# One scan per chunk, 64x64 quarters for two products, a new order of the masks and a spread weight fetch in a linear-attention and mixture-of-experts kernel

## The chip, the cores and the metric

The kernel runs on one core of one Trainium2 chip. The metric is the device time of one execution in microseconds (us); lower is better. Five engines work side by side and wait for each other by semaphores: TensorE (PE, with its weight loads shown as PEld), VectorE (DVE), ScalarE (ACT), GpSimd (POOL) and SyncE (SP), whose queue issues most of the DMA transfers.

## The reference

The first half is a linear attention with a decaying state, for 4 batches, 8 heads, 768 time steps and a head size of 48; the second half sends each of the 3,072 resulting rows of 384 numbers through one of 8 experts.

```python
for t in range(S):                                  # per batch b and head h
    cur = einsum('bhd,bhe->bhde', u[None] * kt, vt)
    y[:, :, t] = einsum('bhd,bhde->bhe', rt, state + cur)
    state = wt[..., None] * state + einsum('bhd,bhe->bhde', kt, vt)
...
skip = x @ w_skip;  do = skip > 0                   # x: y with the heads side by side
e = argmax(x @ w_gate);  g = softmax(x @ w_gate)[e]
out[do] = x[do] + g * (relu(x @ w1[e]) @ w2[e])     # other rows: out = x
```

## The kernel before

**Attention in chunks.** The time steps of a batch are cut into six chunks of 128, so there are 24 chunks, worked off by a loop over `s` (lines 595 to 660). All eight heads of a chunk lie in one tile: head 2a+g has its 48 channels on partitions 64g to 64g+47, and a = 0 to 3 runs along the free dimension with 128 time steps each. For each chunk the kernel needs the products of the decays w.

- `prep_scan` (265) makes `q`, the running product of w from the end of the chunk, with one VectorE scan over 516 columns. `prep_keys` (281) takes the reciprocal `rq` of q's first column in each of four groups, makes `kq` = k*q on GpSimd and, by a second VectorE scan, `rh`, the running product from the start. `prep_reads` (293) makes `rp` = r * rq * rh in four VectorE instructions, and `rk` = r*k on GpSimd, told by `beside` to start after the last of the four. `prep_check` (307) has ScalarE test w and save q's first column.
- `intra` (315) transposes `kq` on TensorE into a PSUM bank of tag psT (ScalarE copies it to `kt`), and multiplies kq by rp into the two banks `psa[0]`, `psa[1]` in 64x64 quarters (328). `mask` (331) copies each bank to SBUF times a triangular mask on VectorE. 
- `bonus_sums` (339) sums u*r*k over the channels by four 128x128 products with `ubk_sb`, which holds u twice on its diagonal blocks and zeros elsewhere, into bank psB; `bonus` (346) multiplies this by v's transpose `vt` into the output bank `psy` on VectorE.
- `outputs` (373) adds to `psy` the masked scores times v (eight products, 378) and, unless the chunk is the first of its batch, four 128x128 products of the state `sblk` with `rp` (383). `sblk` again holds zeros outside its diagonal blocks. `update` (349) adds kt times v to the state in bank psu, and `carry` (361) scales it on ScalarE and copies it to `sblk` in two halves.
- `evict` (386) copies `psy` to `xT`; `rows_out` (390) turns it back into rows and computes the router's logits in one product with `wgp_sb`; `store` (399) copies them out and writes the rows to DRAM.

**Order.** The order on every engine is written by hand (`manual_schedule`): each engine takes its instructions in the order in which the loop issues them. In step `s` the loop stores chunk s-1, updates the state and makes the outputs of chunk s, does the scores, masks, bonus sums and bonus of chunk s+1 and the scans of chunk s+2, and issues the loads of chunk s+4. VectorE's order in a step is therefore scan q, rq, scan rh, rp (chunk s+2), two masks, bonus (chunk s+1). TensorE's is update, outputs (s), transposes, scores, bonus sums (s+1), rows_out (s).

**Router and weights beside it.** After each six chunks a generator `router` (412) is dripped between the other steps, `pace` steps at a time. For the first two groups the one-hot rows are made on ScalarE (`mark`, 479), for the others on VectorE (`one_hot`, 474). Expert weights are fetched in pieces of 1024 columns, one piece a step, at the loop's end (652); they are split into two parts, the high part on ScalarE and the low one on GpSimd (273), one slice a step.

**Queues.** `load_chunk` (140) issues for each chunk two DMAs for w, r and k into one of three buffers and two for `vt` into one of four; `load_v` (157) one for v by rows. With the store and a weight piece all of these go through the SP queue in the order of the loop.

**Experts.** After the loop an early part of expert 0 runs beside the last router group (`early_expert`, 563), and then the experts' products follow (739).

## Time and profile before

| | us |
|---|---|
| median of 3 runs | 317.33 |
| lowest and highest run | 316.35, 317.79 |
| the profiled execution's own time | 317.5 |
| span of the profile (first to last instruction) | 315.6 |
| DVE busy in the span | 244.8 (78%) |
| ACT busy in the span | 185.3 (59%) |
| POOL busy in the span | 115.5 (37%) |

The execution's own time is 1.9 us above the span: what lies before the first and after the last instruction. In 40 slices of the span (7.9 us each), the page gives the busy share of each engine in tenths:

```profile
PE   7499999899898998979999999999999999999992
...
DVE  8899999999999999999637479587785949496310
ACT  4437667689775998766633358274564828184200
POOL 8164455555535566543401772411102020101111
```

The attention takes the first half of the slices, the experts the second. A busy PE is not a PE at its peak, since matmuls are pipelined. The chain of work that ended last, which the next part uses, follows each instruction back to what released it.

### The profile page before, as it was taken

The page shows a single profiled execution, that of the slowest core. Times are in us where ns is not written, and L with a number is a line of the kernel's source. Part 1 is how long each engine was busy: PE and PEld are TensorE (multiplying, and loading weights), DVE is VectorE, ACT ScalarE, POOL GpSimd, SP SyncE. Part 2 cuts the span into 40 slices and gives each one's busy share as a digit, 9 for nine tenths or more (in the row PEclk, how much of TensorE's full clock was granted, in tenths as well). Part 3 has the DMA queues.
Part 4 walks back from the last instruction along what each step waited for, and adds up shares of the span by engine and source line. Part 5 has one row for each costly group of instructions (what it writes and reads, how often), then busy time and mean ns, then how long its engine had stood idle before and what let it go on. Part 6 is the DMA issues. An engine that isn't in the chain of part 4 may idle for free.

```text
span 315.6 us, 8456 instructions
## 1 busy us (share of the span) xinstructions
PE 292.2 (93%) x3229; PEld 269.6 (85%) x3229; DVE 244.8 (78%) x505; ACT 185.3 (59%) x527; POOL 115.5 (37%) x118
## 2 busy tenths in 40 slices
PE   7499999899898998979999999999999999999992
PEld 2388888788787887868889899999999999999991
DVE  8899999999999999999637479587785949496310
ACT  4437667689775998766633358274564828184200
POOL 8164455555535566543401772411102020101111
PEclk9879999999999999999999999999999999999998
DMA  7999999999899988885301489756657473630001
GB/s 227 220 214 241 232 292 271 257 264 264 212 233 257 267 187 179 180 206 194 116 25 34 143 294 348 275 195 218 213 199 239 152 256 95 243 143 27 6 4 37
DMA packets 23778, 60.45 MB, mean 192 GB/s; under 512 B 4902, under 2 KB 11338, under 8 KB 23728
## 3 DMA queue, kind: packets, MB, share of 16 engines
q1 hardware_dynamic: 21248, 53.69, 62.6%
q0 software_dynamic: 2048, 5.48, 5.3%
q8 instruction: 27, 0.44, 0.7%
q10 hardware_dynamic: 432, 0.66, 0.6%
q14 instruction: 23, 0.19, 0.2%
HBM read 52.76 MB, written 7.86 MB: 192 GB/s over the span
## 4 chain that ended last, share of the span: by engine, by line
PE 72%; DMA 13%; DVE 10%; POOL 1%; issue 1%; ACT 1%; SPq 0%; POOLq 0%; DVEq 0%
DMA wrk<-wrk 10%; PE psO L790 7%; PE psO L788 7%; PE psO L789 7%; PE psY L378 6%; PE psH L770 6%; PE psH L769 6%; PE psH L768 6%; PE psA L328 6%; PE psY L383 5%; PE psB L343 5%; DVE asb L334 4%; PE psH L126 4%; DVE psY L347 3%; PE psT L321 3%; DVE rp L297 2%
## 5 line engine op out<-in xcount | busy, mean ns | idle before, releaser
L775 ACT ACTIVATE hh<-psH 128x256 fp32r<-128x256 f32 x60 | 23.0, 383 | 56.8 <-PE psH L770 53.5
L732 POOL DMA_INDIRECT out<-fin,ids x16 | 17.0, 1065 | 102.5 <-DVE fin L795 94.7
L770 PE MATMUL psH<-xTh,w1l 128*128 128x256 f32 x168 | 47.6, 283 | 0.0
L769 PE MATMUL psH<-xTl,w1h 128*128 128x256 f32 x168 | 47.6, 283 | 0.0
L768 PE MATMUL psH<-xTh,w1h 128*128 128x256 f32 x168 | 47.6, 283 | 0.0
L302 POOL TENSOR_TENSOR rk<-wrk 128x512 f32<-128x512 f32 x24 | 30.6, 1275 | 28.9 <-DVE rp L297 14.5
L788 PE MATMUL psO<-w2h,hh 128*128 128x384 f32 x120 | 40.8, 340 | 0.0
L790 PE MATMUL psO<-w2h,hl 128*128 128x384 f32 x120 | 40.2, 335 | 0.0
L789 PE MATMUL psO<-w2l,hh 128*128 128x384 f32 x120 | 40.2, 335 | 0.0
L378 PE MATMUL psY<-asb,v 128*48 128x128 f32 x384 | 26.6, 282 | 13.1 <-DVE psY L347 13.0
L287 POOL TENSOR_TENSOR kq<-wrk,q 128x512 f32<-128x512 f32 x24 | 28.6, 1190 | 18.5 <-DVE q L277 13.4
L776 DVE SCALAR_TENSOR_TENSOR hl<-psH,hh 128x256 fp32r<-128x256 f32 x60 | 25.2, 420 | 12.5 <-ACT hh L775 12.1
L334 DVE TENSOR_TENSOR asb<-psA,c_sb 128x512 f32<-128x512 f32 x48 | 30.7, 681 | 4.3 <-PE psA L328 4.3
L378 PEld LDWEIGHTS psY<-asb,v 128*48 128x48 f32 x384 | 20.5, 126 | 15.6 <-DVE psY L347 15.4
L297 DVE SCALAR_TENSOR_TENSOR rp<-wrk,rq,rh 128x128 f32<-128x128 f32 x96 | 33.1, 405 | 0.5
L770 PEld LDWEIGHTS psH<-xTh,w1l 128*128 128x128 f32 x168 | 32.2, 192 | 0.0
L769 PEld LDWEIGHTS psH<-xTl,w1h 128*128 128x128 f32 x168 | 32.2, 192 | 0.0
L768 PEld LDWEIGHTS psH<-xTh,w1h 128*128 128x128 f32 x168 | 32.2, 192 | 0.0
L795 DVE SCALAR_TENSOR_TENSOR fin<-psO,gates,xg 128x384 f32<-128x384 f32 x15 | 9.3, 618 | 28.5 <-PE psO L790 28.5
L289 DVE TENSOR_TENSOR_SCAN rh<-wrk,pss 128x516 f32<-128x516 f32 x24 | 28.9, 1205 | 2.6 <-PE pss L516 1.3
L277 DVE TENSOR_TENSOR_SCAN q<-wrk,pss 128x516 f32<-128x516 f32 x24 | 29.1, 1214 | 1.4 <-DMA wrk<-wrk 1.4
L343 PE MATMUL psB<-rk,ubk_sb 128*128 128x128 f32 x192 | 27.8, 288 | 0.9 <-POOL rk L302 0.9
(145 smaller groups left out, 668.6 us busy)
## 6 DMA issues: line engine op xcount, KB each, us to landing
r<-w SPq DMA_DIRECT2D x48, 512.0 KB, 5.8
wrk<-wrk SPq DMA_DIRECT2D x46, 288.9 KB, 6.3
v<-vN SPq DMA_DIRECT2D x24, 192.0 KB, 6.2
out<-x SPq DMA_DIRECT2D x24, 192.0 KB, 5.4
vt<-wrk SPq DMA_DIRECT2D x46, 96.0 KB, 6.1
wrk<-wrk SPq DMA_DIRECT2D x1, 258.5 KB, 3.8
wrk<-wrk ACTq DMA_DIRECT2D x1, 256.0 KB, 4.0
wrk<-wrk SPq DMA_DIRECT2D x1, 256.0 KB, 4.5
```

The lines of the kernel that those rows point to most:

```text
L277: nc.vector.tensor_tensor_scan(q.rearrange("p a j -> p (a j)")[:, ::-1], t[:, 1:1 + NP * CW][:, ::-1], floor, 0.0, op0=ALU.mult, op1=ALU.max)
L297: last = nc.vector.scalar_tensor_tensor(rp[:, a], wk["r"][:, a], wk["rq"][:, a], wk["rh"][:, a, :P], op0=ALU.mult, op1=ALU.mult)
L302: mul = nc.gpsimd.tensor_tensor(rk.rearrange("p a j -> p (a j)"), wk["w"][:, R_OFF:K_OFF], wk["w"][:, K_OFF:V_OFF], op=ALU.mult)
L334: nc.vector.tensor_tensor(s, psa[g], tri.rearrange("p (o j) -> p o j", o=1).to_broadcast([P, NP, P]), op=ALU.mult)
L343: nc.tensor.matmul(wk["psb"][:, a], ubk_sb[:, a], wk["rk"][:, a], start=True, stop=True)
L378: nc.tensor.matmul(psy[64 * g:64 * g + D, a], v[:, 2 * a + g], wk["asb"][g][:, a], start=False, stop=(c == 0), skip_group_check=True)
L768: nc.tensor.matmul(ps, w1h[:, o:o + P], xTh[:, kc], start=(kc == 0), stop=False)
L769: nc.tensor.matmul(ps, w1h[:, o:o + P], xTl[:, kc], start=False, stop=False)
L770: nc.tensor.matmul(ps, w1l[:, o:o + P], xTh[:, kc], start=False, stop=(kc == KC - 1))
L788: nc.tensor.matmul(pso, h[j, fc][0], w2h[:, o], start=(fc == 0), stop=False)
L789: nc.tensor.matmul(pso, h[j, fc][0], w2l[:, o], start=False, stop=False)
L790: nc.tensor.matmul(pso, h[j, fc][1], w2h[:, o], start=False, stop=(fc == FC - 1))
```

## The change

**One scan.** The scan `rh`, the small reciprocal `rq` and the four instructions of `rp` go. `prep_keys` takes the reciprocal of all 512 columns of q into `rp`, and `prep_reads` multiplies `rp` by r in place.

```diff
-            nc.vector.reciprocal(rq, wk["q"][:, :, 0:1])
+            rp = wk["rp"] = att.tile([P, NP, P], F32, tag="rp", name=f"rp{i}", bufs=3)
+            nc.vector.reciprocal(rp, wk["q"][:, :, :P])
...
-            nc.vector.tensor_tensor_scan(
-                rh.rearrange("p a j -> p (a j)"), wk["w"][:, 0:NP * CW], floor, 0.0,
-                op0=ALU.mult, op1=ALU.max)
...
-            for a in range(NP):
-                last = nc.vector.scalar_tensor_tensor(
-                    rp[:, a], wk["r"][:, a], wk["rq"][:, a], wk["rh"][:, a, :P],
-                    op0=ALU.mult, op1=ALU.mult)
+            last = nc.vector.tensor_tensor(rp, rp, wk["r"], op=ALU.mult)
```

**Quarters.** `ubk_sb` and `sblk` lose their zero blocks, and the two products that used them become eight products each, of 64 partitions (half g) into 64 output partitions (half c2). Heads are therefore laid out anew: bank `psY`+g holds the heads of half g, with a = 2*c2 + a2. The bonus sums lose their own bank and go into those halves of the score banks' columns that `psb` names.

```diff
-            for a in range(NP):
-                nc.tensor.matmul(wk["psb"][:, a], ubk_sb[:, a], wk["rk"][:, a],
-                                 start=True, stop=True)
+        psb = [z.rearrange("p a (h j) -> p a h j", h=2)[:, :, 1] for z in psa]
...
+            for a2 in range(2):
+                for c2 in range(2):
+                    for g in range(2):
+                        a, rows = 2 * c2 + a2, slice(64 * g, 64 * g + HP)
+                        nc.tensor.matmul(psb[g][64 * c2:64 * c2 + HP, 2 * a2:2 * a2 + 2],
+                                         ubk_sb[rows, a], rk[rows, a], start=True, stop=True)
...
-            nc.vector.tensor_tensor(psy, work[i]["psb"], vt_sb[i % (NBUF + 1)], op=ALU.mult)
+            for g in range(2):
+                work[i]["bonus"] = nc.vector.tensor_tensor(
+                    psy[g][:, :2 * P].rearrange("p (q j) -> p q j", j=HP), psb[g],
+                    vt[:, 4 * g:4 * g + 4], op=ALU.mult)
...
-                for a in range(NP):
-                    nc.tensor.matmul(psy[:, a], sblk[i % 2][:, a], wk["rp"][:, a],
-                                     start=False, stop=True, skip_group_check=True)
+                for a2 in range(2):
+                    for c2 in range(2):
+                        for g in range(2):
+                            a, rows = 2 * c2 + a2, slice(64 * g, 64 * g + HP)
+                            nc.tensor.matmul(psy3[g][64 * c2:64 * c2 + D, a2],
+                                             sblk[i % 2][rows, a, :D], wk["rp"][rows, a],
+                                             start=False, stop=True, skip_group_check=True)
```

With this, `carry` copies the state in one instruction instead of two halves, `evict` copies two half banks, `store` puts its columns back in order, `vt` is loaded by four DMAs of half the size (`load_vt`, one step later than before), and `wgp_sb` by twelve DMAs instead of three in step -2.

**Order.** In step s the bonus sums and the bonus are those of chunk s, not s+1; the transposes (`turn`) are cut off from the scores; `prep_reads` comes behind the masks; `rows_out` of chunk s-1 opens the step.

```diff
                 if on(s - 1):
+                    rows_out(s - 1)
                     store(s - 1)
+                if on(s):
+                    update(s)
+                    carry(s)
+                    bonus_sums(s)
+                drip(pace[0])
...
+                if on(s):
+                    bonus(s)
                 if on(s + 2):
                     prep_scan(s + 2)
+                if on(s + 1):
+                    turn(s + 1)
+                flush()
                 if on(s):
                     outputs(s)
-                flush()
                 if on(s + 2):
                     prep_keys(s + 2)
                     drip(2 * pace[0])
-                    prep_reads(s + 2)
                 if on(s):
                     evict(s)
                 if on(s + 1):
-                    intra(s + 1)
+                    scores(s + 1)
+                    drip(2 * pace[0])
                     mask(s + 1, 0)
                     mask(s + 1, 1)
-                    bonus_sums(s + 1)
-                    bonus(s + 1)
-                    drip(2 * pace[0])
+                if on(s + 2):
+                    prep_reads(s + 2)
                 if on(s + 2):
                     prep_check(s + 2)
```

**Weights and router.** Weight pieces go out at the steps in `FETCH` (k = s - 3) instead of three steps in a row; the slices' split starts one or two steps later. All one-hot rows are made on VectorE (`mark` goes), and the last paces are 3 instead of 2. GpSimd's low part of a slice now waits for the bonus of chunk s instead of the last router instruction.

```diff
+FETCH = (((0, 1), (0, 2, 4)), ((1, 0), (9, 11, 13)), ((0, 0), (10, 12, 14)), ((1, 1), (18, 19, 20)))
...
-                for eq, k0 in (((0, 1), 0), ((0, 0), 3), ((1, 0), 8), ((1, 1), 16)):
-                    if k == k0:
+                for eq, at in FETCH:
+                    if k == at[0]:
                         gens[eq] = load_weights(*eq)
-                    if k0 <= k < k0 + 3:
+                    if k in at:
                         next(gens[eq])
-                if 1 <= k < 7:
-                    split_slice(0, 5 + k, nc.gpsimd)
-                if 9 <= k < 15:
-                    split_slice(1, k - 9, nc.gpsimd)
+                if 2 <= k < 8:
+                    split_slice(0, 4 + k, nc.gpsimd)
+                if 11 <= k < 17:
+                    split_slice(1, k - 11, nc.gpsimd)
```

More of the change, by code (lines that the diff above doesn't have):

```diff
@@ L153, in load_chunk, with load_vt @@
                 nc.sync.dma_start(t[64 * g:64 * g + D], wrk[b, c, g, :, :V_OFF])
-            for g in range(2):
-                nc.sync.dma_start(vf[64 * g:64 * g + D], wrk[b, c, g, :, V_OFF:V_OFF + NP * P])
+        def load_vt(i):
+            b, c = seq[i]
+            vt = vt_sb[i % (NBUF + 1)]
+            for c2 in range(2):
+                for g in range(2):
+                    o = V_OFF + 2 * c2 * P
+                    nc.sync.dma_start(vt[64 * c2:64 * c2 + D, 2 * g:2 * g + 2],
+                                      wrk[b, c, g, :, o:o + 2 * P])
         def load_v(i):
@@ L165, in rwkv_moe_kernel @@
         c_sb = keep.tile([P, C_W], F32, name="c_sb")
-        ubk_sb = keep.tile([P, NP, P], F32, name="ubk_sb")
+        ubk_sb = keep.tile([P, NP, HP], F32, name="ubk_sb")
         u_sb = keep.tile([P, NP], F32, name="u_sb")
@@ L186, in rwkv_moe_kernel @@
         psu = ps1.tile([P, NP, HP], F32, tag="psu", name="psu")
-        psy = ps1.tile([P, NP, P], F32, tag="psY", name="psY")
+        psy = [ps1.tile([P, 512], F32, tag=f"psY{g}", name=f"psY{g}") for g in range(2)]
+        psy3 = [z[:, :2 * P].rearrange("p (b j) -> p b j", b=2) for z in psy]
         psa = [ps1.tile([P, NP, P], F32, tag=f"psA{g}", name=f"psA{g}") for g in range(2)]
-        sblk = [pers.tile([P, NP, 2, HP], F32, name=f"sblk{i}") for i in range(2)]
+        sblk = [pers.tile([P, NP, HP], F32, name=f"sblk{i}") for i in range(2)]
         ohs = keep.tile([P, 1, E], BF16, name="ohs")
@@ L235, in setup @@
             nc.gpsimd.memset(key, 0.5)
-            for g in range(2):
-                rows = slice(64 * g, 64 * g + HP)
-                nc.scalar.copy(ubk_sb[rows, :, rows],
-                               u_sb[rows].rearrange("p (a o) -> p a o", o=1)
-                               .to_broadcast([HP, NP, HP]))
-            nc.tensor.matmul(psy.rearrange("p a j -> p (a j)"), warm[:, :P], warm,
-                             start=True, stop=True, skip_group_check=True)
+            nc.scalar.copy(ubk_sb, u_sb.rearrange("p (a o) -> p a o", o=1)
+                           .to_broadcast([P, NP, HP]))
+            for z in psy:
+                nc.tensor.matmul(z, warm[:, :P], warm, start=True, stop=True,
+                                 skip_group_check=True)
             nc.tensor.matmul(psu.rearrange("p a j -> p (a j)"), warm[:, :P], warm[:, :NP * HP],
                              start=True, stop=True, skip_group_check=True)
-        later, held, marks = deque(), [], deque()
+        later, held = deque(), []
         def flush():
@@ L272, in prep_scan @@
                 lo, raw, hi = lows.pop(0)
-                mul = nc.gpsimd.tensor_tensor(lo, raw, hi, op=ALU.subtract)
-                if vec.last is not None:
-                    beside(mul, vec.last)
+                beside(nc.gpsimd.tensor_tensor(lo, raw, hi, op=ALU.subtract), work[i - 2]["bonus"])
             q = wk["q"] = att.tile([P, NP, CW], F32, tag="q", name=f"q{i}")
@@ L323, in intra, with scores @@
                 nc.scalar.copy(kt, pst)
+        def scores(i):
+            wk = work[i]
             for a in range(NP):
@@ L368, in carry @@
             nb = sblk[(i + 1) % 2]
-            for g in range(2):
-                rows = slice(64 * g, 64 * g + HP)
-                nc.scalar.copy(nb[rows, :, g, :D], psu[rows, :, :D])
+            nc.scalar.copy(nb[:, :, :D], psu[:, :, :D])
         def outputs(i):
@@ L393, in rows_out @@
             px = psx.rearrange("p a j -> p (a j)")
-            for a in range(NP):
-                o = (a // 2) * X2 + (a % 2) * 2 * D
-                nc.tensor.matmul(px[:, o:o + XW], xT[:, a], wgp_sb[:, a], start=(a == 0),
-                                 stop=(a == NP - 1), skip_group_check=True)
+            for q in range(4):
+                o = (q // 2) * X2 + (q % 2) * 2 * D
+                nc.tensor.matmul(px[:, o:o + XW], xT[:, q], wgp_sb[:, q], start=(q == 0),
+                                 stop=(q == 3), skip_group_check=True)
         def store(i):
@@ L574, in early_expert @@
                 hfs.append((h0l[:, fs], hf, h0h[:, fs].bitcast(F32)))
-            pso = ps1.tile([P, DM], F32, tag="psB", name="psO0")
+            pso = ps1.tile([P, DM], F32, tag="psY1", name="psO0")
             w2h, w2l = wsp[0, 2], wsp[0, 3]
@@ L752, in expert @@
             for q in range(nh):
-                ps = ps1.tile([P, CAP], F32, tag=("psA0", "psA1", "psY", "psB")[q % 4],
+                ps = ps1.tile([P, CAP], F32, tag=("psA0", "psA1", "psY0", "psY1")[q % 4],
                               name=f"psH{e}_{q}")
```

130 lines of the change are left out of this document (58 added, 72 removed).

## The prediction

> **What bounds the kernel now.** I read the page first, then the chain of waits for the extent of the attention, the busy time of that stretch, one step of it, and the DMAs.
>
> ```profile
> span 315.6 us, 8456 instructions
> PE 72%; DMA 13%; DVE 10%; POOL 1%; issue 1%; ACT 1%; SPq 0%; POOLq 0%; DVEq 0%
> ...
> 16.05 1.95 PE psY L378 x16
> ...
> 163.16 0.59 ACT xT L388
> ...
> 16.05:163.16 147.11, 137.82 (x2092) 120.66 (x2093) 135.56 (x280) 105.57 (x345) 75.00 (x69) 0.99 0.90 219
> ```
>
> The chain runs from the first product into `psy` at 16.05 us to the last copy out of it at 163.16: 147.1 us for 24 chunks, 6.13 us each. In this stretch (last row: PE, PEld, DVE, ACT, POOL, clock, DMA share, GB/s) PE is busy for 137.8 us and DVE for 135.6, so two engines are nearly full, and the page's 10% for DVE is no measure of what DVE sets. An undisturbed step, first DVE by the timeline (start, us), then PE by the chain:
>
> ```profile
> 28.27 1.22 DVE L277 TENSOR_TENSOR_SCAN q<-wrk,pss 128x516 f32<-128x516 f32 x1
> 29.52 0.18 DVE L284 RECIPROCAL rq<-q 128x4 f32<-128x4 f32 x1
> 29.62 1.20 DVE L289 TENSOR_TENSOR_SCAN rh<-wrk,pss 128x516 f32<-128x516 f32 x1
> 30.85 1.14 DVE L297 SCALAR_TENSOR_TENSOR rp<-wrk,rq,rh 128x128 f32<-128x128 f32 x4
> 32.35 1.29 DVE L334 TENSOR_TENSOR asb<-psA,c_sb 128x512 f32<-128x512 f32 x2 [0.35 <-PE psA L328]
> 33.55 0.69 DVE L347 TENSOR_TENSOR psY<-psB,vt 128x512 f32<-128x512 f32 x1
> ```
> ```profile
> 29.74 1.09 PE psY L383 x8
> 30.82 0.44 PE psT L321 x4
> 31.26 1.02 PE psA L328 x24
> 32.28 1.09 PE psB L343 x8
> 33.37 0.87 PE psX L396 x8
> 34.24 0.49 PE psu L356 x16
> 34.74 0.88 PE psY L378 x16
> ```
>
> PE's seven groups follow each other without a gap and sum to 5.88 us: that is the period. DVE has 0.35 us to spare in it, so router steps and disturbances push it over, and the mean becomes 6.13. A gain needs both engines to become shorter.
>
> **VectorE.** Start to start, a step now takes 1.25 (scan q) + 0.10 (rq) + 1.23 (rh) + 1.14 (rp) + 1.20 (masks) + 0.60 (bonus) = 5.5 us, the wait aside. Gone are rq, rh and the old rp, 2.47. New are a reciprocal of 512 columns and a product of two SBUF tiles of 512.
>
> ```profile
> L96 DVE TENSOR_TENSOR w1l<-r,w1h 128x512 fp32r<-128x512 f32 x36 | 24.9, 693 | 2.1
> ...
> L205 DVE RECIPROCAL gate<-sm x4: 164/182/191, 64.2 to 167.0; 128x6 f32<-128x6 f32 x4
> ...
> L284 DVE RECIPROCAL rq<-q x24: 178/179/181, 6.4 to 150.2; 128x4 f32<-128x4 f32 x24
> ```
>
> The product has its like in the 0.69 us of L96. The reciprocal is the unknown: the trace has it at 4 columns (178/179/181 ns) and 6 (164/182/191). The medians differ by 3 ns for two columns, 1.5 ns a column: 0.18 + 508 x 1.5 ns = 0.94 us. From 178 to 191 it would be 6.5 ns: 3.5 us, the far end; the near end is no slope at all, 0.18. I take the rate of the nearest large elementwise row, (693 - 179)/508 = 1.0 ns a column, 0.69 us. The bonus becomes two instructions of 256 columns, 0.18 + 252 x 1.0 ns = 0.43 each, 0.77 together with the 0.1 us by which neighbours overlap (rows 29.52 and 29.62). Start to start: 1.25 + 0.60 + 1.20 + 0.60 + 0.70 = 4.35 us.
>
> To this come router steps. They are all on one line, 205, and the same stretch has for that line's DVE time:
>
> ```profile
> 16.05:163.16 147.11, 10.22 (x52) 0.99 0.90 219
> ...
> L205 DVE TENSOR_SCALAR hot<-iota,rall 128x256 bf16<-128x256 bf16 x12 | 2.6, 283 | 0.1
> ```
>
> 10.2 us, with 12 one-hot rows more at 0.28 (the second row), 3.4 us: 13.6/24 = 0.57 a step. DVE: 4.9 us a step.
>
> **TensorE.** Quarter-size products run side by side, but not for nothing. Scores (L328) are 64x64 quarters too: each of the four array quarters gets four streams of 128 columns or of 64, at most 512 columns, in 1.02 us. The weight queue idles where the shape of the products changes, as before L343:
>
> ```profile
> PEld psB L343 <- issue: 3.4, 20, 0.2
> ```
>
> 20 times 0.17 us. So scores are 0.17 + 0.85, 1.66 ns a column with four quarters side by side. Bonus sums give each quarter two streams of 128 columns: 0.43 + 0.17 = 0.60, and the state's part the same, instead of 1.09 each (0.43 to 0.85 are the ends, the full overlap without the shape change and the time of all sixteen scores). The order adds shape changes: rows_out and the transposes now follow quarters (+0.17 each), scores follow the state's quarters and save it. New step: 0.87 + 0.17 (rows_out), 0.49, 0.60, 0.44 + 0.17, 0.88, 0.60, 0.85: 5.07 us.
>
> The Trainium skill, TensorEngine Tiling (Array Packing), Key Properties, says that a change of tiling mode, as against one of tile, drains the engine, and that tiles of one mode run independently; by its four tiles at once without that drain each product would be 0.43 here, and the step 0.5 us shorter. The 0.17 us of the row is the drain's price here, so I keep it.
>
> **The new wait.** Bonus sums share banks with the scores, so they wait for both masks, and everything behind them on PE waits too. Count from the scores' end: masks from 0.07 to 1.35 (two of 0.68, overlapping), and PE does rows_out and update meanwhile, 1.53: the wait is covered by 0.1 us, and would cost what the masks run longer. Bonus sums end at 2.13. DVE does rp until 1.95, then a router step, then the bonus from 2.2: first bank at 2.6, second at 2.96. PE's transposes last until 2.74 and the first bank's products until 3.2, so the second bank is ready. Outputs, state and scores end at 5.07; DVE's scan and reciprocal are then done at 4.9 with router steps behind. Everything fits with 0.1 to 0.2 us to spare, so I add 0.18 for steps where it doesn't: 5.25 a step, 24 x (5.25 - 6.13) = **-21.1 us**.
>
> GpSimd's low part of a weight slice now waits for the bonus, with kq queued behind it: at about the 1.23 us of kq's row further down it runs from 2.96 to 4.2, where the scan's end releases kq anyway, and kq is needed only in the next step. ScalarE loses a half copy and the one-hot rows and gets one more eviction of half the size; with 105.6 us busy in 147 it has room.
>
> **What comes back.** First, DMA. Bytes a chunk (KB each):
>
> ```profile
> r<-w SPq DMA_DIRECT2D x48, 512.0 KB, 5.8
> wrk<-wrk SPq DMA_DIRECT2D x46, 288.9 KB, 6.3
> v<-vN SPq DMA_DIRECT2D x24, 192.0 KB, 6.2
> out<-x SPq DMA_DIRECT2D x24, 192.0 KB, 5.4
> vt<-wrk SPq DMA_DIRECT2D x46, 96.0 KB, 6.1
> ...
> 37.00:57.00 20.00, 19.59 (x314) 17.22 (x312) 19.21 (x42) 14.43 (x48) 10.61 (x9) 1.00 1.04 267
> ```
>
> 2 x 288.9 + 2 x 96 + 192 + 192 KB = 1.18 MB a chunk, 1.71 with a weight piece. In the stretch of six weight pieces in a row DMA moves 267 GB/s at a share of 1.04, full: 4.4 us for a plain step, 6.4 for one with a piece. Spread pieces (steps 3, 5, 7) average 5.4, just hidden. But `FETCH` interleaves two tensors at k = 9 to 14, steps 12 to 17: six pieces in a row again, 6 x (6.4 - 5.25) = 6.9 us of backlog, less some 3 us by which loads run ahead: **+3.9**. The last three pieces meet no chunk loads.
>
> Second, contention of DVE and POOL:
>
> ```profile
> 111.38 2.16 DVE L297 SCALAR_TENSOR_TENSOR rp<-wrk,rq,rh 128x128 f32<-128x128 f32 x4
> 111.63 1.23 POOL L287 TENSOR_TENSOR kq<-wrk,q 128x512 f32<-128x512 f32 x1
> ```
>
> Beside kq the rp group takes 2.16 us, not 1.14. In the new order rp stands behind the masks, where kq is done; the router's one-hot rows can still meet POOL: **+1.5** in all.
>
> Third, the start. SP goes through 2 more `vt` DMAs a chunk and nine more for `wgp_sb`. The queue holds only so many:
>
> ```profile
> 63.95 6.65 DMA wrk<-wrk
> ...
> 70.62 7.75 DMA wrk<-wrk
> ...
> 65.73 0.78 SPq L155 DMA_DIRECT2D vt<-wrk  x2
> 66.60 0.38 SPq L160 DMA_DIRECT2D v<-vN  x1
> 67.07 0.38 SPq L410 DMA_DIRECT2D out<-x  x1
> 67.50 0.44 SPq L90 DMA_DIRECT2D r<-w  x1
> 70.01 0.94 SPq L153 DMA_DIRECT2D wrk<-wrk  x2
> ...
> wgp_sb<-wgp SPq DMA_DIRECT2D x1, 9.0 KB, 4.4
> ```
>
> The load issued at 63.95 lands at 70.60, and the second `wrk` of 70.01 goes out at 70.62: between them lie the other wrk half, two vt, v, out, r and one wrk, so at most eight DMAs are in flight. The smallest of `wgp_sb`'s takes 4.4 us to land (last row), so twelve keep the queue for 12 x 4.4/8 = 6.6 us, and three for 1.7; behind them lie the load of chunk 3 and, by the data, rows_out of chunk 0, which I put 1.5 us late, the rest hidden by the first scores: **+1.5**. The first output itself moves little (one scan less, loads 1 us later).
>
> The experts' part keeps its work. Sum against the profiled execution: 317.5 - 21.1 + 3.9 + 1.5 + 1.5 = **303.3 us**; the median of the runs is 0.2 lower. Forecast 303, and by the step's error of 0.25 us (24 x 0.25 = 6) and the DMA term its own range is 296 to 309.
>
> **Rivals.** (a) **DMA stays the bound.** A chunk has 8 DMAs, 9 with weights, and eight fit. If SP's order or smaller rows keep steps near 5.6 and weight steps near 6.4, the attention takes 12 x 5.6 + 12 x 6.4 = 144 less the pieces without loads, a gain of 1 to 9: 309 to 317. For it: the share of 1.04, and 6 us to landing. Against: most of that time is waiting behind other bytes, and the bytes are the same. 0.14.
>
> (b) **The landing time is fixed and not a queue's**: with 8 in flight and 6.3 us each, a plain step is 6.3 us and one with a piece 9/8 x 6.3 = 7.1: 161 us, +14: 331, slower. It decides from 6.1 us a landing. Against: `r` of 512 KB and `vt` of 96 KB would not both need 6 us if bytes didn't queue, but do so behind each other. 0.06.
>
> (c) **The reciprocal is slow.** If the engine needs eight passes for each column, it is 0.18 + 508 x 8 x 1.0 ns = 4.2 us, DVE's step is 8.4, and 24 x (8.4 - 6.13) = +55: about 371. It decides from 1.9 us on (4.9 + 1.2 = 6.1), 3.4 ns a column. For it: 179 ns at 4 columns leave room for 8 ns each. Against: two more columns would add 16 ns, and the medians differ by 3. 0.07. The Trainium skill, VectorE: DVE Perf Modes, First, the fixed hardware budget, says that reciprocal runs as an iterative divide with a repeat count of 8; the two rows speak against eight passes a column, but no row here is wide enough to decide.
>
> (d) **Better than reckoned**, the quarters hide their shape changes and DMA runs ahead: 24 x 5.0 = 120, no backlog: below 296, say 292. 0.08.
>
> (e) The quarters run one after the other: 8 x 128 x 1.66 ns = 1.7 us a product, a step of 7.3, 345. The scores' row excludes it nearly: 0.01.
>
> **Numbers.** Forecast 0.64 (296 to 309), (a) 0.14, (b) 0.06, (c) 0.07, (d) 0.08, (e) 0.01. The range 293 to 316 holds the forecast, most of (a) and half of (d): 0.64 + 0.13 + 0.04 = 0.81. A measurement of this kernel tells 0.5% from no change (315.7 to 318.9). Faster: 0.64 + 0.11 + 0.08 = 0.83; same, the upper edge of (a): 0.03; slower, (b), (c) and (e): 0.14.
>
> **What would show it.** The reciprocal near 0.7 us and rp near 0.69; about 0.6 us for each of the two products in quarters; scores start to scores start about 5.2 us in plain steps; waits of PE for the masks or for the bonus below 0.3 us a step; SP's waits on landings in steps 12 to 17. It is wrong if the reciprocal's row is above 1.9 us, if PE waits over 0.5 us a step for DVE, or if scans wait for `wrk`.

## The result: 15% slower

The changed kernel takes 365.88 us (median of 4 runs, 364.9 to 368.16) beside 317.56 for the kernel before on the same chip: a ratio of 1.154, 95% interval 1.147 to 1.160. The forecast was 303, the range 293 to 316. Further on, a ratio leaves out runs over 1.5% above their kernel's fastest of the same set, which on the chip of e4 to e7 leaves two of the thirteen runs of the kernel before (321.19 and 323.05 us; the others took 326.97 to 328.76), and in e14's later set on that chip all eleven (326.84 to 328.78). From the profile of the changed kernel, first the busy times and the costliest group of the page (behind the bar: busy us in all, mean ns of one, idle us before):

```profile
PE 308.9 (85%) x3582; PEld 272.5 (75%) x3582; DVE 281.3 (77%) x445; ACT 170.3 (47%) x506; POOL 113.5 (31%) x117
...
L285 DVE RECIPROCAL rp<-q 128x512 f32<-128x512 f32 x24 | 80.5, 3353 | 0.8
```

The reciprocal takes 3,353 ns, not 690. A step without router work, by VectorE's timeline (start, us, line, what it makes, in brackets the idle time before it):

```profile
58.08 1.22 DVE L277 TENSOR_TENSOR_SCAN q<-wrk,pss 128x516 f32<-128x516 f32 x1
59.33 3.35 DVE L285 RECIPROCAL rp<-q 128x512 f32<-128x512 f32 x1
62.60 1.22 DVE L331 TENSOR_TENSOR asb<-psA,c_sb 128x512 f32<-128x512 f32 x2
63.74 0.68 DVE L293 TENSOR_TENSOR rp<-rp,wrk 128x512 f32<-128x512 f32 x1
64.64 0.76 DVE L351 TENSOR_TENSOR psY<-psA,vt 128x256 f32<-128x256 f32 x2 [0.21 <-issue]
65.31 1.22 DVE L277 TENSOR_TENSOR_SCAN q<-wrk,pss 128x516 f32<-128x516 f32 x1
```

VectorE is busy nearly without a gap for 7.23 us, scan to scan; before it was 5.88. TensorE now waits for it, and pays twice. Its timeline in this step and the following one:

```profile
63.38 1.16 PE L345 MATMUL psA<-rk,ubk_sb 64*64 64x128 f32 x16 [1.39 <-DVE asb L331]
...
65.23 1.95 PE L384 MATMUL psY<-asb,v 128*48 128x128 f32 x16
...
71.58 1.17 PE L345 MATMUL psA<-rk,ubk_sb 64*64 64x128 f32 x16 [1.28 <-DVE asb L331]
...
73.33 1.08 PE L384 MATMUL psY<-asb,v 128*48 128x128 f32 x16
```

The bonus sums wait 1.39 and 1.28 us for the masks, which stand behind the reciprocal. The same sixteen products then take 1.95 us once and 1.08 the next time: the granted clock reads 0.50 from 65 to 68 us and 1.00 around 73. The mean granted clock of the execution is 0.898 (0.986 before). The last products of `rows_out`, by the view of the tile psX (min/median/max ns, first and last start), for the changed kernel:

```profile
L407 PE MATMUL psX<-wgp_sb,xT x192: 274/275/542, 22.0 to 212.7; 128*128 128x105 f32 x192
```

and for the kernel before:

```profile
L396 PE MATMUL psX<-wgp_sb,xT x192: 255/275/358, 21.4 to 164.7; 128*128 128x105 f32 x192
```

The attention ends 48.0 us later; the profiled executions differ by 366.46 - 317.5 = 49.0. Nearly all of the loss is in the attention.

### The profile page after: what moved, and what is told of

Same layout as the page of the kernel before. It is cut to its first block, busy times and chain, and to the rows that moved or that the text cites. A ratio compares the mean times of both kernels' runs of the same rounds, so it can differ in the third digit from the quotient of the medians.

```text
span 364.7 us, 9180 instructions
## 1 busy us (share of the span) xinstructions
PE 308.9 (85%) x3582; PEld 272.5 (75%) x3582; DVE 281.3 (77%) x445; ACT 170.3 (47%) x506; POOL 113.5 (31%) x117
## 4 chain that ended last, share of the span: by engine, by line
PE 45%; DVE 8%; DMA 1%; issue 1%; POOL 1%; ACT 0%; POOLq 0%; DVEq 0%
PE psO L794 6%; PE psO L795 6%; PE psO L796 6%; PE psH L776 6%; PE psH L775 6%; PE psH L774 6%; DVE rp L285 4%; PE psH L127 3%; PE psX L407 2%; DVE q L277 2%; PE psY L384 1%; PE psX L733 1%; DVE psY L351 1%; DMA xg<-out,idr 1%; PE psA L325 1%
## 5 line engine op out<-in xcount | busy, mean ns | idle before, releaser
L285 DVE RECIPROCAL rp<-q 128x512 f32<-128x512 f32 x24 | 80.5, 3353 | 0.8
L345 PE MATMUL psA<-rk,ubk_sb 64*64 64x128 f32 x384 | 26.2, 324 | 27.7 <-DVE asb L331 22.9
L738 POOL DMA_INDIRECT out<-fin,ids x16 | 17.1, 1066 | 102.5 <-DVE fin L801 94.7
L345 PEld LDWEIGHTS psA<-rk,ubk_sb 64*64 64x64 f32 x384 | 15.7, 154 | 33.9 <-issue 24.3
L384 PE MATMUL psY<-asb,v 128*48 128x128 f32 x384 | 34.6, 337 | 3.8 <-DVE psY L351 3.7
L399 ACT COPY xT<-psY 128x256 f32<-128x256 f32 x48 | 15.7, 376 | 43.0 <-PE psY L392 41.6
L384 PEld LDWEIGHTS psY<-asb,v 128*48 128x48 f32 x384 | 26.4, 153 | 10.7 <-DVE psY L351 10.4
L325 PE MATMUL psA<-rp,kq 64*64 64x128 f32 (+1 forms) x768 | 30.6, 284 | 2.2 <-DVE rp L293 2.2
```

Source lines behind the costliest of these rows:

```text
L285: nc.vector.reciprocal(rp, wk["q"][:, :, :P])
L325: nc.tensor.matmul(psa[g][j:j + HP, a, j:], wk["kq"][rows, a, j:j + HP], wk["rp"][rows, a, j:], start=True, stop=True)
L345: nc.tensor.matmul(psb[g][64 * c2:64 * c2 + HP, 2 * a2:2 * a2 + 2], ubk_sb[rows, a], rk[rows, a], start=True, stop=True)
L384: nc.tensor.matmul(psy3[g][64 * c2:64 * c2 + D, a2], v[:, 2 * a + g], wk["asb"][g][:, a], start=False, stop=(c == 0), skip_group_check=True)
```

## The experiments

Two readings stood against each other. **The reciprocal** alone: everything else gains as forecast. **The rest too**: order, start or DMAs lose what they were to gain. A ratio is always to the kernel before on the same chip, with its 95% interval. Some chips take about 10 us longer than the first in the experts' part: from the last rows_out to the end of the span it is 151 us before and 152 after on the first, 162 in e7 and in m1_widths, which are the kernel before with a small edit, on others. So stretches of the attention are compared in the traces, one profiled execution of each kernel. The table is worked out from the starts of the q scans in each trace (us): when chunk 3's begins, from there to chunk 20's (17 steps), from there to chunk 23's, and the last start of rows_out.

| kernel | scan 3 | 3 to 20 | 20 to 23 | last rows_out | ratio |
|---|---|---|---|---|---|
| before | 22.5 | 106.8 | 19.7 | 164.7 | 1 |
| after | 28.4 | 134.4 | 32.1 | 212.7 | 1.154 |
| e1_two_scans | 27.7 | 110.4 | 28.1 | 180.7 | 1.058 |
| e2_reciprocal_alone | 24.8 | 126.1 | 24.0 | 191.4 | 1.079 |
| e3_max_instead | 28.0 | 103.9 | 28.9 | 175.1 | 1.044 |
| e4_fewer_dmas | 26.0 | 96.7 | 27.7 | 164.8 | 1.019 |
| e9_pieces_in_a_row | 23.9 | 101.6 | 27.7 | 167.4 | 1.007 |
| e10_after_fewer_dmas | 25.6 | 134.4 | 31.5 | 209.5 | 1.141 |
| e13_quarters_products_behind | 22.2 | 100.6 | 25.6 | 161.8 | not settled |
| e14_flush_ahead_of_carry | 23.1 | 102.5 | 21.8 | 160.8 | 0.990 |

### The reciprocal by itself

In m1_widths the kernel before takes five reciprocals more, in `setup`:

```diff
+            for w in (8, 32, 64, 128, 256):
+                nc.vector.reciprocal(sblk[1].rearrange("p a g j -> p (a g j)")[:, :w],
+                                     smask.rearrange("p a j -> p (a j)")[:, :w])
```

> The kernel before with five more reciprocals in the setup, of 8, 32, 64, 128 and 256 columns, into a tile that is cleared afterwards: the cost of a column by itself. If each column costs 6.2 ns at any width (3.35 us less 0.15 over 512), they take 0.20, 0.35, 0.55, 0.95 and 1.75 us; if the slow rate belongs to wide ones or to q's values and strides, the narrow ones stay near 0.2 and the 256 columns near 0.45.

Its groups by shape (behind the first bar: busy us in all, then the mean of one in ns):

```profile
L287 DVE RECIPROCAL rq<-q 128x4 f32<-128x4 f32 x24 | 4.3, 179 | 0.8
L220 DVE RECIPROCAL sblk<-smask 128x256 f32<-128x256 f32 x1 | 1.8, 1753 | 0.0
L220 DVE RECIPROCAL sblk<-smask 128x128 f32<-128x128 f32 x1 | 1.0, 952 | 0.0
L205 DVE RECIPROCAL gate<-sm 128x6 f32<-128x6 f32 x4 | 0.7, 180 | 0.0
L220 DVE RECIPROCAL sblk<-smask 128x64 f32<-128x64 f32 x1 | 0.6, 553 | 0.0
L220 DVE RECIPROCAL sblk<-smask 128x32 f32<-128x32 f32 x1 | 0.4, 353 | 0.0
L220 DVE RECIPROCAL sblk<-smask 128x8 f32<-128x8 f32 x1 | 0.2, 203 | 0.0
```

A straight line: (1753 - 203)/248 = 6.25 ns a column, 153 ns before the first; at 512 columns 3,353 ns, the row of the changed kernel to the nanosecond, and at 4 columns 178. The six-column rows with a median of 182 don't lie on it (191 would), only their maximum does; why the others are shorter no run shows.

In e2_reciprocal_alone the kernel before takes over the reciprocal and the one product, and nothing else:

```diff
-            nc.vector.reciprocal(rq, wk["q"][:, :, 0:1])
-            nc.vector.tensor_tensor_scan(rh...)
+            nc.vector.reciprocal(rp, wk["q"][:, :, :P])
...
-            for a in range(NP):
-                last = nc.vector.scalar_tensor_tensor(rp[:, a], ...)
+            last = nc.vector.tensor_tensor(rp, rp, wk["r"], op=ALU.mult)
```

> The kernel before with only the wide reciprocal and the product by r in place of the small reciprocal, second scan and four instructions; order, full products and fetch as before. Theory R: VectorE's step is 5.5 - 2.47 + 3.35 + 0.60 = 7.0 plus 0.4 for the router, 24 x (7.4 - 6.13) = +30: about 345 to 350. Theory O: near 320, since the old order is kept.

354.24 us, 1.079 (1.075 to 1.083): plain steps of 7.04 us, and the prediction's 5.5 - 2.47 with 3.39 for the reciprocal and 0.61 for the product, start to start, make 7.03. On the chip of this run 1.079 is 26 us; by the traces the attention ends 26.7 us later.

In e1_two_scans the changed kernel gets both scans and the old rp back, behind the masks, and keeps the rest:

```diff
-            nc.vector.reciprocal(rp, wk["q"][:, :, :P])
+            nc.vector.reciprocal(rq, wk["q"][:, :, 0:1])
+            nc.vector.tensor_tensor_scan(rh...)
...
-            last = nc.vector.tensor_tensor(rp, rp, wk["r"], op=ALU.mult)
+            for a in range(NP):
+                last = nc.vector.scalar_tensor_tensor(rp[:, a], ...)
```

> The changed kernel with the first part undone: the small reciprocal, the second scan and the four instructions for rp are back (rp still behind the masks); quarters, order and fetch stay. Theory R (the wide reciprocal, 3.35 us, is what costs): a step of VectorE is 1.25 + 0.10 + 1.23 + 1.14 + 1.20 + 0.60 + 0.57 for the router = 6.1 at most, less where nothing waits; the time comes down by 24 x about 2.2 = 53 us, to 308 to 318. Theory O (the new order, with bonus sums in the score banks behind both masks, costs by itself): it stays above 330.

346.98 us, 1.058 (1.050 to 1.066). So the reciprocal isn't all: without it the rest is still slower than before. In e3_max_instead the reciprocal's place is taken by an instruction of the length that the prediction had reckoned; the division is left out, rp is r times q:

```diff
-            nc.vector.reciprocal(rp, wk["q"][:, :, :P])
+            nc.vector.tensor_tensor(rp, wk["q"][:, :, :P], floor..., op=ALU.max)
```

> The changed kernel with the wide reciprocal replaced by an elementwise maximum of q and the floor in PSUM, 512 columns, about 0.69 us: the division is left out, rp is r times q, and the routing follows other values. It is the cost that the prediction took for the reciprocal. Theory R: what the prediction summed for the rest, 303, plus a start that is some 5 us later than reckoned (the trace of the changed kernel issues chunk 3's load at 22.5 us instead of 14.4): 302 to 310. Theory O: above 320.

341.83 us, 1.044 (1.039 to 1.048), with the stand-in at 0.69 us. **Both readings hold**: the reciprocal takes 37.6 us of the attention (212.7 - 175.1), and what is left is 4.4% slower, not 4.5% faster.

### The DMAs

The chain of waits of e3 near the end (start, us, what):

```profile
125.54 6.32 DMA wrk<-wrk
...
131.93 0.33 SPq L158
...
132.31 6.73 DMA wrk<-wrk
...
139.11 0.33 SPq L158
...
139.49 6.19 DMA wrk<-wrk
```

One load a step stands in the chain: it is issued, lands 6 us later, and only then does SP's queue go on to the next chunk's. In e4_fewer_dmas the same bytes come in fewer DMAs, since the host lays the second copy of v and `wgp` out in the new order:

```diff
-                for g in range(2):
-                    o = V_OFF + 2 * c2 * P
-                    nc.sync.dma_start(vt[64 * c2:64 * c2 + D, 2 * g:2 * g + 2],
-                                      wrk[b, c, g, :, o:o + 2 * P])
+                nc.sync.dma_start(vf[64 * c2:64 * c2 + D],
+                                  wrk[b, c, c2, :, V_OFF:V_OFF + NP * P])
...
+                    nc.sync.dma_start(wgp_sb, wgp)
```

> The kernel of e3_max_instead (its division is still left out), but the host lays the second copy of v and wgp out in the new order, so that a chunk's vt comes in two DMAs instead of four and wgp in one instead of twelve; the bytes are the same. In e3 the step in the middle of the attention was 5.9 us, the scan of chunk 3 started 5.6 us later than before, and the whole was 13.7 us above the kernel before. Theory N (the number of DMAs binds: eight in flight, each some 5 to 6 us from issue to landing, nine or ten to a chunk): steps fall to about 5.3 us (-13 us in 20 steps) and the start gives 4 back: 322 to 328 us, a ratio of 0.98 to 1.0 to the kernel before. Theory B (the bytes bind, 1.2 to 1.7 MB a step): only the start is mended, 336 to 339 us, a ratio of 1.025 to 1.035. A third, W (PE and VectorE take turns around the shared psA banks, and the loop is as long as that chain): also only the start, but then hardly a scan waits for wrk.

328.31 us, 1.019 (1.010 to 1.027). By the traces the attention ends 10.3 us earlier than in e3: 2.0 of them are won ahead of chunk 3, 7.2 in the 17 steps. By the ratios the gain is 2.5%, but e4's stands beside the two shortest runs of the kernel before; beside the median of all thirteen, 327.78, e4 is level. Its plain step on TensorE, products of the outputs to the same products of the next chunk:

```profile
25.86 1.08 PE L381 MATMUL psY<-asb,v 128*48 128x128 f32 x16
26.87 0.65 PE L389 MATMUL psY<-rp,sblk 64*48 64x128 f32 x16
27.34 1.04 PE L322 MATMUL psA<-rp,kq 64*64 64x128 f32 x32
28.31 1.14 PE L404 MATMUL psX<-wgp_sb,xT 128*128 128x105 f32 x8
29.38 0.56 PE L359 MATMUL psu<-v,kt 128*48 128x48 f32 x16
29.88 0.67 PE L342 MATMUL psA<-rk,ubk_sb 64*64 64x128 f32 x16
30.48 0.66 PE L312 MATMUL psT<-c_sb,kq 128*128 128x128 f32 x4
31.14 1.08 PE L381 MATMUL psY<-asb,v 128*48 128x128 f32 x16
```

The groups follow each other without a gap, 5.28 us in all. Its five steps from chunk 3 to 8 take 5.17 to 5.29 us each, beside the forecast's 5.25. e7_before_more_dmas does the opposite to the kernel before:

```diff
-                nc.sync.dma_start(vf[64 * g:64 * g + D], wrk[b, c, g, :, V_OFF:V_OFF + NP * P])
+                for h in range(2):
+                    nc.sync.dma_start(vf[64 * g:64 * g + D, 2 * h * P:2 * (h + 1) * P],
+                                      wrk[b, c, g, :, V_OFF + 2 * h * P:V_OFF + 2 * (h + 1) * P])
```

> The kernel before with one edit: each chunk's vt comes in four DMAs of half the width instead of two (eight and nine DMAs a chunk instead of six and seven), the same bytes. Theory N: eight in flight at 5 to 6 us each give a step of 5.5 to 6.5 us, so steps with a weight piece become later and the kernel takes 3 to 9 us more (a ratio of 1.01 to 1.03). Theory B: no difference that can be measured (0.997 to 1.004).

331.77 us, 1.020 (1.005 to 1.035); by the traces the attention ends 3.3 us later (168.0): in the direction of the number of DMAs. Both edits also halve or double the length of a row that a DMA moves, so the runs don't tell whether it is the eight in flight or the smaller rows.

e9_pieces_in_a_row is e4 with the old fetch of the weights:

```diff
-FETCH = (((0, 1), (0, 2, 4)), ((1, 0), (9, 11, 13)), ((0, 0), (10, 12, 14)), ((1, 1), (18, 19, 20)))
+FETCH = (((0, 1), (0, 1, 2)), ((0, 0), (3, 4, 5)), ((1, 0), (8, 9, 10)), ((1, 1), (16, 17, 18)))
```

> The kernel of e4_fewer_dmas with the weights fetched as in the kernel before (three pieces in a row, at steps 0, 3, 8 and 16 after the first, and the slices split as there). Plain steps of e4 take 5.28 us, those of chunks 9 to 12 and 14 to 18 take 5.6 to 6.4, beside spread pieces. Theory S (the interleaved spread costs, as the prediction had it with 3.9 us): 3 to 6 us below e4, a ratio of 1.0 to 1.01. Theory B (the bytes cost the same in any order): within 2 us of e4.

320.13 us, 1.007 (1.004 to 1.011). By the ratios it gains about 3.5 us on e4, whose ratio rests on two runs of the kernel before; by the traces it loses 4.9 in the 17 middle steps and gains 2.2 ahead of chunk 3, where no weight is fetched yet, and its attention ends 2.6 later. The two chips differ by more than that, so the effect of the spread is not settled; a loss of the spread's in the middle is not to be seen.

e10_after_fewer_dmas gives the changed kernel itself, reciprocal and all, the layout of e4 (the diff above).

> The changed kernel itself, reciprocal and all, with the host's layout of e4 (two DMAs for vt, one for wgp): the full computation. Theory R (the reciprocal's 3.35 us make VectorE the bound, and the DMAs lie beside it): steps stay at 7.2 to 8.2 us, only the start gains, a ratio of 1.14 to 1.155 (the changed kernel has 1.154). Theory A (the two losses add up, since e4 took 13.5 us off e3): a ratio of 1.10 to 1.12.

362.49 us, 1.141 (1.135 to 1.146): 3.2 us at the end of the attention, 2.8 of them won ahead of chunk 3, where the same edit brought 10.3 beside the quick stand-in. While VectorE needs 7.2 us a step, the loads have time. The losses don't add up: each bound hides a part of the other.

### The router in the queues

e4 takes 27.7 us for its last three steps, the kernel before 19.7. VectorE of e4, with the router in its queue:

```profile
135.42 1.28 DVE L328 TENSOR_TENSOR asb<-psA,c_sb 128x512 f32<-128x512 f32 x2
136.62 0.68 DVE L290 TENSOR_TENSOR rp<-rp,wrk 128x512 f32<-128x512 f32 x1
138.94 0.41 DVE L503 TENSOR_TENSOR sg<-oh,vals 128x240 bf16<-128x240 bf16 x1 [1.64 <-POOL vals L500]
139.26 0.76 DVE L348 TENSOR_TENSOR psY<-psA,vt 128x256 f32<-128x256 f32 x2
139.93 1.22 DVE L273 TENSOR_TENSOR_SCAN q<-wrk,pss 128x516 f32<-128x516 f32 x1
```

and TensorE:

```profile
137.34 0.66 PE L312 MATMUL psT<-c_sb,kq 128*128 128x128 f32 x4
141.20 0.19 PE L510 MATMUL pss<-tab,identb 128*128 128x40 bf16 x1 [3.20 <-DVE q L273]
...
141.75 1.95 PE L381 MATMUL psY<-asb,v 128*48 128x128 f32 x16
143.63 1.10 PE L389 MATMUL psY<-rp,sblk 64*48 64x128 f32 x16
144.52 1.92 PE L322 MATMUL psA<-rp,kq 64*64 64x128 f32 x32
```

A router step waits for GpSimd; the bonus stands behind it. A router product waits for the scan, which reads `floor` in the same bank; the outputs, ready 1.2 us earlier, stand behind it. Then the products run at half the clock: the busy times of a plain stretch and of that one (last three columns: granted clock, DMA share, GB/s; the plain one is the last chunk of a batch, which has no update):

```profile
41.70:46.88 5.18, 5.18 (x92) 4.09 (x93) 4.63 (x9) 2.93 (x12) 2.35 (x3) 1.00 1.06 291
141.82:146.43 4.61, 4.61 (x66) 3.90 (x65) 0.84 (x2) 1.57 (x6) 0.94 (x2) 0.50 0.02 4
```

(2.5 us of e4's excess belong to the stand-in, which reads that bank too and waited 1.82 and 0.72 us for router copies and products.) The following runs move this work. e5_router_later is e4 with the router's steps behind the scan and behind rp:

```diff
-                drip(pace[0])
...
                     prep_scan(s + 2)
+                drip(pace[0])
...
-                    drip(2 * pace[0])
                     mask(s + 1, 0)
                     mask(s + 1, 1)
                 if on(s + 2):
                     prep_reads(s + 2)
+                if on(s + 1):
+                    drip(2 * pace[0])
```

> As e4_fewer_dmas, and the router's steps moved behind the scan and behind rp, so that none stands ahead of the masks or the bonus in VectorE's queue (in e3 the last four scans came 28.9 us after one another where before they took 19.7, with router steps of 1.5 us ahead of the masks and 1.6 us of waiting ahead of the bonus). Theory W (what stands ahead of masks and bonus lengthens the loop one for one): 5 to 9 us below e4. Theory V (VectorE's sum is what counts, and it doesn't matter where a step stands): within 2 us of e4.

334.47 us, 1.028 (1.014 to 1.042); in the profiled run, of 329.12 us, the attention is as long as in e4 (164.9): moving alone brings nothing. e8_router_behind puts them behind the outputs and behind rp, and the cast of iota on GpSimd two steps later, out of the way of chunk 1's kq; the stand-in is q times r:

```diff
                     outputs(s)
+                drip(pace[0])
...
                     prep_reads(s + 2)
+                if on(s + 1):
+                    drip(4 * pace[0] if on(s + 2) else 2 * pace[0])
...
+                if s == 0:
                     nc.gpsimd.tensor_copy(iota, c_sb[:, C_IOTA:C_IOTA + 2 * P])
```

> The kernel of e4_fewer_dmas with its order mended where its trace shows losses against the kernel before: the scan of chunk 3 starts 3.6 us later (GpSimd's first kq stands behind a cast of iota that waits for a load, and TensorE's first outputs stand behind the transposes that wait for kq), and the last three scans take 8.0 us longer (router steps ahead of masks and bonus on VectorE, router products ahead of the outputs on TensorE, the clock at a half after each pause). Here the cast comes two steps later, and the router's steps stand behind the outputs and behind rp alone. The stand-in for the reciprocal is q times r, so that it no longer reads the bank that holds the router's sums; the division is left out, and rp is r times r times q. Theory O (order at start and end is what is left of the miss): 8 to 12 us below e4, a ratio of 0.98 to 0.995. Theory V (VectorE's sum or the bytes set these stretches, wherever the steps stand): a ratio of 1.01 to 1.03.

325.44 us, 1.025 (1.021 to 1.029). The start is mended (chunk 3's scan at 21.5 us, 23.9 in e9 on the same chip), the router's steps cost more: 27.5 us for the last three and 108.4 for the 17 before them, and the attention ends at 171.6.

e6_quarters_acts_r is e1 with e4's layout, and ScalarE takes r times 1/q0:

```diff
+            for a in range(NP):
+                nc.scalar.activation(rr[:, a], wk["r"][:, a], AF.Copy, scale=rq[:, a])
...
+            last = nc.vector.tensor_tensor(rp, wk["rr"], wk["rh"][:, :, :P], op=ALU.mult)
```

> The kernel of e1_two_scans (both scans, no wide reciprocal, the full computation) with the host's layout of e4 and r times 1/q0 taken by ScalarE, so that rp is one product of 512 columns on VectorE. VectorE's step is 1.25 + 0.10 + 1.23 + 0.60 + 1.20 + 0.70 + 0.57 = 5.65 us, PE's 5.1. If the number of DMAs was what held the changed order back: 24 x (5.7 - 6.13) = -10 us, 314 to 322 us on this chip, a ratio of 0.96 to 0.98, faster than both kernels. If the bytes or the turns of PE and VectorE bind: 328 to 338 us, a ratio of 1.0 to 1.03.

336.31 us, 1.030 (1.014 to 1.046); plain steps take 6.06 us, since the four products stand ahead of the eviction on ScalarE and rows_out waits. e11_quarters_order puts them behind it and takes over e8's order:

```diff
                     evict(s)
+                if on(s + 2):
+                    scale_r(s + 2)
```

> The kernel of e6_quarters_acts_r (both scans, ScalarE takes r times 1/q0, the full computation) with the order of e8_router_behind, and ScalarE's eviction of psY ahead of its products with r: in e6 rows_out waited 0.8 us a step for the eviction behind them, and plain steps took 6.06 us. If that was the step's bound, plain steps fall to 5.4 to 5.6, and with start and end mended the ratio is 0.96 to 0.985, faster than both kernels. If VectorE's sum is the bound, steps stay at 5.8 to 6.1 and the ratio is 1.0 to 1.02.

333.91 us, 1.052 (1.048 to 1.057): plain steps fall to 5.22 us, the steps from chunk 8 on take 5.4 to 12.3, as uneven as in e8 (5.3 to 11.8). e12 and e13 leave the router's VectorE steps where the change has them and hold its TensorE products back until bonus sums and outputs are issued; `small` is VectorE throughout:

```diff
                     bonus_sums(s)
+                flush()
                 drip(pace[0])
...
-                flush()
                 if on(s):
                     outputs(s)
+                flush()
```

> The kernel of e4_fewer_dmas with the early start of e8 (the cast of iota later, q times r in place of the reciprocal, so the division is left out and rp is r times r times q), the router's VectorE steps where the changed kernel has them, but the router's products on TensorE behind the bonus sums and behind the outputs instead of ahead of rows_out and ahead of the outputs, and its small steps on VectorE instead of GpSimd. Theory Q (what was left of the miss is TensorE standing still behind router products that wait for VectorE and GpSimd, and then running at half the clock): the last three scans come in some 22 us instead of 27.7, the start gives 4, and the ratio is 0.96 to 0.985, near the forecast of 0.955. Theory V (the router's own time on VectorE is what counts): the last three scans stay above 26 us and the ratio is 0.99 to 1.01 (the start alone).

> The same order of the router's products and the same start, on the full computation: the kernel of e11_quarters_order (both scans, ScalarE takes r times 1/q0 behind the eviction; its plain steps took 5.22 us, its steps with router work 7 to 12) with the router's steps back where the changed kernel has them. Theory Q: a ratio of 0.965 to 0.99, faster than both kernels. Theory V: a ratio of 1.0 to 1.03.

e12 328.52 us and e13 326.67 beside 327.59, where the kernel before varied from 321.05 to 328.68, so neither is told apart from it; by the traces the attention ends as before in e12 (164.7) and 2.9 us earlier in e13 (161.8). The last three steps take 23.5 us in e12, between its two expectations, and 25.6 in e13. e12's 17 steps before them take 105.2, e4's 96.7; its stand-in, lengthened beside GpSimd (below), has a part in that. In e13's last steps one long wait of VectorE is left, for a copy that stands behind the carry on ScalarE:

```profile
139.92 0.18 DVE L509 TENSOR_TENSOR vals<-gd,vals 128x6 bf16<-128x6 f32 x1 [2.10 <-ACT vals L506]
```

e14_flush_ahead_of_carry moves that flush ahead of `update` and `carry`:

```diff
                     store(s - 1)
+                flush()
                 if on(s):
                     update(s)
                     carry(s)
                     bonus_sums(s)
-                flush()
                 drip(pace[0])
```

> The kernel of e13_quarters_products_behind (full computation) with one edit: the router's held products and copies are issued ahead of the state's update and of ScalarE's four products of the carry, instead of behind the bonus sums. In e13 the last three scans came in 25.6 us (before: 19.7, forecast of the plain step: 15.7), and in them VectorE stood 2.1 us ahead of a bonus for a copy of vals that stood behind the carry on ScalarE, and 0.5 us for the exponentials. Theory Q (the router's waits, handed from engine to engine, are what is left): 2 to 4 us less in the last three scans, a ratio of 0.97 to 0.99. Theory V (the router's own steps on VectorE between scan and masks, 1.6 and 1.8 us, set it): within 1 us of e13's 25.6, and a ratio of 0.985 to 1.01.

**325.23 us beside 328.31, 0.990 (0.988 to 0.993).** Against the changed kernel that is a clear gain. Against the kernel before it is 1% beside the eleven runs made with it, and not settled: two earlier runs of the kernel before on this chip (321.19 and 323.05 us) were shorter than all six of e14. By the traces e14's attention ends 3.9 us earlier than before (160.8 beside 164.7). The last three steps take 21.8 us, 3.8 less than in e13: the waits were worth that there. Of this, 1.0 us is left at the end of the attention, since chunk 3 begins 0.9 later than in e13 and the 17 steps take 1.9 longer; whether the edit does that or the run, no trace shows. What remains in the last three steps is mostly VectorE's own sum, busy for 20.2 of 21.8 us; one of these steps, 7.43 us scan to scan, has ten router instructions between the two scans and 0.26 us of idle time:

```profile
125.57 1.22 DVE L273 TENSOR_TENSOR_SCAN q<-wrk,pss 128x516 f32<-128x516 f32 x1
...
127.27 1.23 DVE L286 TENSOR_TENSOR_SCAN rh<-wrk,pss 128x516 f32<-128x516 f32 x1 [0.26 <-ACT tab L529]
...
132.33 0.77 DVE L357 TENSOR_TENSOR psY<-psA,vt 128x256 f32<-128x256 f32 x2
133.00 1.22 DVE L273 TENSOR_TENSOR_SCAN q<-wrk,pss 128x516 f32<-128x516 f32 x1
```

## Why the prediction was wrong

**The reciprocal's term was mis-sized: 0.69 us put down, 3.35 measured.** This is the step that failed. Its own bounds held the truth: "from 178 to 191 it would be 6.5 ns: 3.5 us, the far end". It chose the elementwise rate because two medians lay 3 ns apart; m1 shows that the maximum of the six-column rows lies on the line of all other widths and the median does not. Four columns against six were no ground for a factor of 128 in width. Rival (c) had the mechanism, with a chance of 0.07, 4.2 us and a time of 371. Two of the prediction's own signs of being wrong came true: the reciprocal above 1.9 us, and TensorE waiting for VectorE over 0.5 us a step (1.39 and 1.28 us in the two steps shown). The Trainium skill, VectorE: DVE Perf Modes, First, the fixed hardware budget, has the reciprocal as an iterative divide with a repeat count of 8; the trace agrees in kind, with 6.25 ns a column against 1.0 for a product.

With 3.35 us in its place the prediction's sum comes to 4.9 + 2.66 = 7.56 us a step and 317.5 + 24 x (7.56 - 6.13) = 352 us, or 359 with its three terms for DMA, contention and start. The measured 366 is 14 above 352; the start (5.9 us late) and the last three steps (32.1 us instead of 3 x 7.56 = 22.7) would make 15.

**The plain step's size was right, partly by luck.** It was put at 5.25 us, of which 5.07 were TensorE's work and 0.18 waits. With a quick stand-in (e4) it is 5.28, all of it work. Start to start, the bonus sums take the 0.60 that was forecast and the state's part 0.47 instead of 0.60; the output products take 1.01 instead of 0.88 and the scores 0.97 instead of 0.85. The allowance for waits covered what the work had too little. The second scan and the old rp do drop out of VectorE's step as reckoned: e2's sum of 7.03 us meets 7.04. No run has the quarters in the old order, or the new order without the quarters, so what each is worth alone is not shown.

**DMA: the mechanism was named, the price too low, and the wrong part suspected.** The prediction put +3.9 on the spread fetch and trusted that "the bytes are the same" against rival (a). With a quick stand-in the number or the smallness of the DMAs for `vt` and `wgp` alone costs 10.3 us (e3 to e4), while a loss by the spread is not to be seen in e9; the forecast of 303 would have failed with a reciprocal of 0.69 us too: e3 ends the attention 10.4 us later than before (up to 3.8 of them the stand-in's own waits), not 14 earlier. In the changed kernel as it stands the same thing costs 3.2 us.

**The start** was put at +1.5. Chunk 3's scan is 5.9 us late in the changed kernel, 3.6 in e4 with one DMA for `wgp_sb` and two for `vt`, and in the pair on one chip 1.4 us late in e9 and 1.0 early in e8. What e8 takes away was not named in the prediction: chunk 1's kq waits on GpSimd behind a cast. It does so in the kernel before, too (it starts at 16.5 us there and at 16.8 in the changed kernel), but in the new order the first outputs stand on TensorE behind kq's transposes.

**The last steps** had no term of their own. The sum spread the router evenly, 0.57 us a step. But masks, bonus sums, bonus, outputs and scores now form one ring through two engines and two banks, and what waits ahead of one of them in a queue holds up the others; then TensorE stands and loses half its clock. This reading fits the runs but is not shown by itself: moving the router's VectorE steps left 26.4 to 30.4 us for the last three (e5, e8, e11), holding its TensorE products back gave 21.8 to 25.6 (e12, e13, e14). The three steps from 20 to 23 take 32.1 us in the changed kernel, where three plain ones are 3 x 7.23 = 21.7. From e13 to e14, waits worth 3.8 us go; what is left there is mostly VectorE's.

## What to carry to other kernels

A price extrapolated over two orders of magnitude is no price: take the far end as the forecast's rival with a chance to match, or choose the instruction whose wide form the trace has already shown. When the same bytes come in more DMAs, count DMAs and the length of their rows, not bytes alone. When two engines hand work to and fro over shared banks, look at what stands ahead of each hand-over in the in-order queues, side work above all, before adding up busy times.

## What the runs showed of the hardware

**A reciprocal costs 153 ns and 6.25 ns for each column** of fp32, at seven widths from 4 to 512 columns (m1 and the changed kernel); single rows came out shorter, down to 164 ns at six columns (before) and 138 at four (e11).

**A small VectorE instruction can last as long as the GpSimd instruction beside it.** In e12, where kq runs beside the stand-in q times r, an addition of 54 columns took 1.19 us and ended 0.06 us after kq; the same one in the changed kernel, after the reciprocal had outlasted kq, took 0.15. e12:

```profile
51.22 0.98 DVE L281 TENSOR_TENSOR rp<-q,wrk 128x512 f32<-128x512 f32 x1
52.13 1.19 DVE L426 TENSOR_TENSOR lg<-lgs 128x54 f32<-128x54 f32 x1
```

its GpSimd at that time:

```profile
51.62 1.64 POOL L284 TENSOR_TENSOR kq<-wrk,q 128x512 f32<-128x512 f32 x1
```

and the changed kernel:

```profile
69.83 0.15 DVE L430 TENSOR_TENSOR lg<-lgs 128x54 f32<-128x54 f32 x1
```

The Trainium skill, GPSIMD Engine Reference, Specifications, says that GpSimd shares its SBUF interface with VectorE and contends with instructions of two SBUF inputs; the rows agree, and the reciprocal, of one input, was never lengthened beside kq (3,352 to 3,354 ns in all 24).

**TensorE's granted clock falls to a half around its waits, and short ones are enough.** In e4 it reads 0.50 from 139.7 to 146.4 us, around a wait of 3.2 us that ends at 141.2, with sixteen products at 1.95 us instead of 1.08. In the changed kernel it reads 0.50 from 65 to 68 us, after a wait of 1.39 us that ends at 63.4; after the next, of 1.28 us, it stays at 1.00. So these runs give no length of a pause from which on it falls.
